# Weight conversion on another engine, two more blocked parts of GEMM 2, and weight tiles shared by alternating rows, in a fused attention and feed-forward kernel

## The chip, the cores and the metric

One core of a Trainium2 chip. The metric is the device time of one execution in microseconds (us), of which the median of several runs is given. TensorE (PE) does matrix products into PSUM, VectorE (DVE), ScalarE (ACT) and GpSimd (POOL) work element by element, and SyncE (SP) starts the transfers between device memory and SBUF. GpSimd can't read PSUM.

## What is computed

Random-feature attention over 8 batches, 8 heads, 576 tokens of 64, and then a feed-forward layer over the 4608 x 512 result:

```python
def phi(x):                                   # x scaled by 64 ** -0.25
    proj = einsum('bhsd,md->bhsm', x, omega)  # 128 features
    h = proj - sum(x * x, -1) / 2
    return exp(h - max(h, -1)) / sqrt(128)
kv = einsum('bhsm,bhsd->bhmd', phi(k), v);  z = sum(phi(k), 2)
x = (phi(q) @ kv) / (phi(q) @ z + 1e-6)       # then to 4608 x 512
h = x @ w_in                                  # GEMM 1: 512 -> 2048
g = h * erf(softplus(h))
out = g @ w_out                               # GEMM 2: 2048 -> 512
```

Inputs and output are float32 but the two weight matrices, which come as float64.

## The kernel before

**Precision.** Each factor of the large products is split in a rounded high part and a rest, both in TensorE's fast float32 format, and each product is three matmuls: high x high, high x rest, rest x high.

**Super-blocks.** The tokens are worked off in six super-blocks (`SUPERS`, line 31) of two halves each, 288, 288, 432, 432, 432 and 432 columns a half. A super-block needs the attention of its tokens to be done, so the attention of later batches (32 pairs of heads) is spread over the GEMMs of earlier super-blocks. GEMM 1 and GEMM 2 go in four quarters q of d_ff; GEMM 2 of a quarter runs beside GEMM 1 of the next (`second`, called with `last`).

**Seven products.** The first three super-blocks do GEMM 1 plainly: for each pair of d_ff tiles and model halves, eight products of blocks. The others take a 2 x 2 block product in seven products (`PRODUCTS`, line 59) of sums of blocks: of the weights S1 to S4, of the right sides T1 to T4. GEMM 2 does the same where `blocked(b, q)` holds: in super-block 4, and in super-block 5 but for its last quarter, seven parts in all. A blocked part makes its right sides in `pieces2`: four differences of half-blocks of g (`gsum`), and high and rest of B21 with B22, of B11, of T1 with T2 and of T3 with T4. It takes its seven products for each of two rows j, whose steps alternate (`merged`).

**Weights.** In super-block 0 each of 32 weight units of 128 x 512 float64 is loaded raw (`st`, as low and high 32-bit words) and turned into float32 by `make` (line 412): `pbias` on ScalarE takes the high word into PSUM with another exponent (`wt`), `ptail` on GpSimd takes the three top bits of the low word, `pjoin` on VectorE shifts one and adds the other bits, `phigh` on ScalarE rounds, `prest` on VectorE subtracts; the result `w` is also stored in device memory (`wdw`). Later uses fetch it from there. The sums S1 to S4 are made by `make_sums` (line 451) from the two weight tiles as they are used in a plain product: those of GEMM 1 in super-block 2, those of GEMM 2 in super-block 3 (`SUMS2`). They are stored too (`wdc`). A blocked product fetches single blocks of 256 KB, and `lease` (line 741) puts two of one row in a tile `wb`, in the groups of `UNITS`.

**Order.** `build` only lists operations with their reads, writes, due times, and possible engines with a duration in us and a slack for each; `Plan.order` (line 151) then simulates the engines with these durations and writes down the order in which every engine's queue gets its instructions. Each queue runs strictly in that order on the chip. Loads are counted as bytes at 270 GB/s and 2.3 us. For the tail the plan has

```python
pl.op("ptail", [("G", 0.95, -1e9)], lambda e: E.w_tail(st), ...
```

Tiles take slots of named pools; `SLOTS` and `CAPS` (lines 78 to 80) bound how many a stream may hold. The pool `w` has 8 slots for weight tiles (`w`, at most 6 up to the end of super-block 3, then 8), raw weights and sums together (`st`, 2), the float32 copies for sums (`wt`, 1) and the rounded sums (`cv`, 2).

Of the kernel before, what the change touches and what calls it, by code (L numbers as in the profile page):

```python
# [14 lines left out]
ALU = mybir.AluOpType  # L15
# [17 lines left out]
FROM = tuple(2 * sum(t for t, _ in SUPERS[:i]) for i in range(len(SUPERS) + 1))  # L33
BLOCKED = 4
SUMS2 = BLOCKED - 1
SUMS = max(i for i, (_, plain) in enumerate(SUPERS) if plain)
# [29 lines left out]
            ("X", "A22", "T4", (1, 0), 0))  # L66
UNITS = (("A11", "S1"), ("S2", "S4"), ("S3", "A12"), ("A22",))


def blocked(b, q):  # L70

    return b >= BLOCKED and (b < len(SUPERS) - 1 or q < NQ - 1)

# [239 lines left out]


AHEAD = 40.0

# [27 lines left out]
def build(emit):  # L344
# [28 lines left out]
    for i in range(len(SUPERS)):  # L373
        starts.append(starts[-1] + per[i] + more[i] * PAIR)

    def pair_time(n, x):
        b, p = divmod(n, NP)
        if b <= need[0]:
            return n * FIRST + x * 14.0
        i = next(i for i in range(len(SUPERS)) if need[i] >= b)  # L380
        each = (starts[i] - starts[i - 1]) / more[i - 1]
        k = (need[i] + 1) * NP - n
        return starts[i] - LEAD - k * each + x * min(each, 33.0) * 1.2
# [18 lines left out]
    def parts(t, src, keys, banked=False):  # L402

        ks = range(2)
        pl.op("phigh" if banked else "whigh", [("A", 0.63, -1e9)] + [("G", 0.7, WHG)] * (not banked),
              lambda e: E.w_high(e, t, src),
              reads=keys, writes=[(t, ("h", k)) for k in ks])
        pl.op("prest" if banked else "wrest", [("V", 0.68, -1e9)] + [("G", 1.3, 3.0)] * (not banked),
              lambda e: E.w_rest(e, t, src),
              reads=keys + [(t, ("h", k)) for k in ks], writes=[(t, ("l", k)) for k in ks])  # L410

    def make(u, t):

        nm = "_".join(str(c) for c in u)
        st = pl.tile("w", f"st{nm}", [P, HW, 2], I32, "st")
        pl.op("wload", [("S", 0.1, AHEAD)], lambda e: E.w_load(st, u),
              writes=[(st, "h"), (st, "l"), (t, "room")], size=P * HW * 8)
        w = pl.tile("ps", f"wt{nm}", [P, HW], I32, "wp")
        pl.op("pbias", [("A", 0.67, -1e9)], lambda e: E.w_bias(e, st, w),
              reads=[(st, "h")], writes=[(w, 0)])  # L420
        pl.op("ptail", [("G", 0.95, -1e9)], lambda e: E.w_tail(st), reads=[(st, "l")], writes=[(st, "l")])
        pl.op("pjoin", [("V", 0.68, -1e9)], lambda e: E.w_join(st, w), reads=[(st, "l"), (w, 0)],
              writes=[(w, 0)])
        parts(t, lambda: w.ap.bitcast(F32).rearrange("p (k c) -> p k c", k=2), [(w, 0)], True)
        store(u, t)

    def room():
        count[0] += 1
        return CAPS["w"] if clock[0] < starts[max(SUMS, SUMS2) + 1] else SLOTS["w"]

# [20 lines left out]
    def make_sums(key, t0, t1):  # L451
# [3 lines left out]
        for i, t in enumerate((t0, t1)):  # L455
            pl.op("wwhole", [("V", 0.68, -1e9), ("G", 1.3, 3.0)],
                  lambda e, i=i, t=t: E.w_whole(e, r.ap[:, i], t),
                  reads=[(t, (x, k)) for x in "hl" for k in range(2)], writes=[(r, i)])
        s = pl.tile("w", "S" + nm, [P, 4, BW], F32, "st")

# [125 lines left out]
    def key_values(n, t0):  # L586
        a = pairs[n]
        f, v = a["fk"], a["v"]
        kvp = a["kvp"] = pl.tile("ps", "kvp" + a["nm"], [P, 512], F32, "att", early(n))
        for j in range(2):  # L590
            pl.op("kv", [("T", (5 - j) * COST["kv"], -1e9)], lambda e, j=j: E.key_values(kvp, f, v, j),
                  reads=[(f, i) for i in range(NC)] + [(v, 0)], writes=[(kvp, 0)],
                  plan=pair_time(n, t0 + 0.08 * j))
        whole = n < WHOLE
        kh = a["kh"] = pl.tile("kh", "kh" + a["nm"], [P, 2, P], F32 if whole else F32R)
        kl = a["kl"] = kh if whole else pl.tile("kl", "kl" + a["nm"], [P, 2, P], F32R)
        pl.op("kvhigh", [("V", 0.6, -1e9), ("A", 0.7, -1e9)], lambda e: E.kv_high(e, kh, kvp),
              reads=[(kvp, 0)], writes=[(kh, 0)])
        if not whole:
            pl.op("kvrest", [("V", 0.6, -1e9)], lambda e: E.kv_rest(kl, kvp, kh),  # L600
                  reads=[(kvp, 0), (kh, 0)], writes=[(kl, 0)])

    def turn(n, t0):
        a = pairs[n]
        whole = n < WHOLE
        lent = ("g", "qh0", 2) if n < NP else ("qh", "qh", None)
# [12 lines left out]
    def attend(n, t0):  # L619
        a = pairs[n]  # L620
        for t, (c0, w) in enumerate(SPANS):
            rc = pl.tile(f"rc{t}", f"rc{a['nm']}_{t}", [P, w])
            nds = [pl.tile("ps", f"nd{a['nm']}_{j}_{t}", [P, 512], F32, "att", early(n)) for j in range(2)]
            for j, nd in enumerate(nds):
                c = range((j * S + c0) // 384, (j * S + c0 + w - 1) // 384 + 1)
                pl.op("nd", [("T", w / 600 if n < WHOLE else 3 * max(0.111, 0.012 + w / 2400), -1e9)],
                      lambda e, j=j, c0=c0, w=w, nd=nd:
# [112 lines left out]

    def lease(where, src, wn):

        if wn not in where:
            us = next(x for x in UNITS if wn in x)
            t = blocks([src(x) for x in us])
            where.update({x: (t, i) for i, x in enumerate(us)})
        return where[wn]

    def gemm1(b, ph, fp):
        T, d = SUPERS[b][0], drain(b)  # L750
        hs = pl.tile("g", f"hs{b}_{ph}_{fp}", [P, 2, 2, T], F32, "hs")
        gran[b, ph, fp] = {"hs": hs}
        where, banks = {}, {}

        def one(bank, wn, xn, to, plus):
            w = lease(where, sources(ph, fp), wn)
            first = bank not in banks
# [98 lines left out]

    def gemm2_blocks(b, q, j):
        T, d = SUPERS[b][0], drain(b)
        where, banks = {}, {}
        src = sources2(q, j)  # L860
        for i in range(2):
# [3 lines left out]
        def one(bank, wn, xn, to, plus):  # L865
            u, k = lease(where, src, wn)
            first = bank not in banks
# [21 lines left out]
    def gemm2(b, q, et):  # L889
# [16 lines left out]
        def one(t, f):  # L906
            if not ops:
                ops.extend(pl.tile("ps", f"o{b}_{q}_{et}_{i}", [P, 512], F32, "moe2",
                                   6 if b == len(SUPERS) - 1 else None) for i in range(2))
                w.append(weights2(q // 2, et, q % 2))  # L910
                if b == SUMS2 and any(blocked(x, q) for x in range(len(SUPERS))):
                    beside[q, et] = w[0]
                    if et >= KH:
                        make_sums(("2", q, et - KH), beside[q, et - KH], w[0])
# [20 lines left out]
    def second(b, q, e):  # L935
        if not blocked(b, q):
            merged([gemm2(b, q, (0, 2, 1, 3)[e])])
        elif not e:
            merged([gemm2_blocks(b, q, j) for j in range(KH)])

# [9 lines left out]
    for b in range(len(SUPERS)):  # L950
        plain = SUPERS[b][1]
        length = (starts[b + 1] - starts[b]) / NQ
        for q in range(NQ):
# [5 lines left out]
            for block in (("f", 0), ("e", 0), ("e", 1), ("e", 2), ("e", 3)):  # L959
                what, x = block  # L960
                if what == "f":
                    gs = range(GP * q, GP * q + GP)
                    merged([(plain1 if plain else gemm1)(b, *divmod(g, FP)) for g in gs])
                    chain(b, gs)
# [12 lines left out]
def tile_attention_moe(ctx: ExitStack, tc: tile.TileContext, qT, kT, qR, kR, qN, kN, vP, omT, w1, w2, out):  # L977
# [68 lines left out]
    class Emit:  # L1046
# [11 lines left out]

        def w_tail(self, t):
            x = t.ap[:, :, 0]  # L1060
            pool.tensor_scalar(x, x.bitcast(mybir.dt.uint32), 2.0 ** -29, 7.0, op0=ALU.mult, op1=ALU.min)

# [288 lines left out]
```

## Time and profile before

| | |
|---|---|
| median of 3 runs | 1058.01 us (1057.6 to 1059.11) |
| profiled execution | 1057.43 us |
| its span, first to last instruction | 1055.6 us, mean granted clock 0.996 |
| TensorE matmul busy | 1028.8 us (97%), 6748 matmuls |
| TensorE weight load busy | 972.6 us (92%) |
| VectorE busy | 786.2 us (74%) |
| ScalarE busy | 690.4 us (65%) |
| GpSimd busy | 617.1 us (58%) |
| DMA | 220.08 MB, 208 GB/s on average |

Matmuls overlap and their ends are modelled, so TensorE's busy time shows where it had nothing to do, not how fast it was. The granted clock is the share of 2.4 GHz that the chip gave TensorE. In the tables of stretches the busy times are in us, in the order matmul, weight load, VectorE, ScalarE, GpSimd. All instructions carry the same line, that of a helper, so groups are told by their tiles: `h`, `hX`, `hY`, `hZ` are banks of GEMM 1, `o`, `oX`, `oY`, `oZ` of GEMM 2, `nd`, `pp`, `pt`, `kvp` of the attention, `hs` and `gs` hold h and its gate, `th`, `tl`, `bh`, `bl`, `bb` right sides of blocked parts, `os` the output sums, `xs` the attention's output, `qh` its turned features, `R` and `S` the float32 copies and the sums of weights. The stretch from 54 to 216 us holds super-block 0 with 26 of the 32 conversions of weights; 340 to 533 is super-block 2, 533 to 733 super-block 3, after that the last two. A wait names what released it last; a queue runs in order, so whatever stands behind a waiting instruction waits as well.

### The profile page before, as it was taken

The page shows a single profiled execution, that of the slowest core. Times are in us where ns is not written, and L with a number is a line of the kernel's source. Part 1 is how long each engine was busy: PE and PEld are TensorE (multiplying, and loading weights), DVE is VectorE, ACT ScalarE, POOL GpSimd, SP SyncE. Part 2 cuts the span into 40 slices and gives each one's busy share as a digit, 9 for nine tenths or more (in the row PEclk, how much of TensorE's full clock was granted, in tenths as well). Part 3 has the DMA queues.
Part 4 walks back from the last instruction along what each step waited for, and adds up shares of the span by engine and source line. Part 5 has one row for each costly group of instructions (what it writes and reads, how often), then busy time and mean ns, then how long its engine had stood idle before and what let it go on. Part 6 is the DMA issues. An engine that isn't in the chain of part 4 may idle for free.

```text
span 1055.6 us, 18596 instructions
## 1 busy us (share of the span) xinstructions
PE 1028.8 (97%) x6748; PEld 972.6 (92%) x6748; DVE 786.2 (74%) x1316; ACT 690.4 (65%) x1300; POOL 617.1 (58%) x436
## 2 busy tenths in 40 slices
PE   7999898999999999999999999999999999999998
PEld 7799788999999999999989999999999999899997
DVE  5767666886777766747787797879887778888664
ACT  8878786776666665664856575758657575635550
POOL 6668756642345755625765264738895688686520
PEclk9999998999999999999999999999999999999999
DMA  8366667587445576446446666666776656677662
GB/s 241 121 207 212 220 244 254 209 308 247 149 160 196 180 238 237 158 159 201 138 156 233 212 214 226 222 202 215 252 268 224 224 179 191 225 267 231 227 209 80
DMA packets 87962, 220.08 MB, mean 208 GB/s; under 512 B 9920, under 2 KB 10432, under 8 KB 87872
## 3 DMA queue, kind: packets, MB, share of 16 engines
q1 hardware_dynamic: 87712, 218.83, 61.8%
q8 instruction: 54, 0.88, 0.4%
q14 instruction: 36, 0.29, 0.1%
q10 hardware_dynamic: 160, 0.07, 0.0%
HBM read 175.87 MB, written 42.99 MB: 207 GB/s over the span
## 4 chain that ended last, share of the span: by engine, by line
PE 82%; DVE 7%; POOL 5%; issue 2%; ACT 2%; DMA 1%; SPq 0%; POOLq 0%; DVEq 0%; ACTq 0%
PE o L994 22%; PE h L994 15%; PE hX L994 9%; PE oX L994 6%; PE kvp L994 5%; PE nd L994 5%; PE ppq L994 4%; PE hY L994 4%; PE ppk L994 4%; PE oY L994 3%; PE hZ L994 2%; PE pt L994 2%; PE oZ L994 1%; POOL st L994 1%; POOL hs L994 1%
## 5 line engine op out<-in xcount | busy, mean ns | idle before, releaser
L994 PE MATMUL o<-gh,w 128*128 128x432 f32 (+1 forms) x1088 | 281.9, 332 | 0.8 <-ACT os L994 0.7
L994 PE MATMUL h<-xh,w 128*128 128x288 f32 (+1 forms) x768 | 199.5, 328 | 3.3 <-DVE w L994 1.9
L994 PEld LDWEIGHTS o<-gh,w 128*128 128x128 f32 x1088 | 192.6, 188 | 6.7 <-ACT os L994 0.9
L994 PE MATMUL o<-gl,w 128*128 128x432 f32 (+1 forms) x544 | 178.7, 329 | 0.1
L994 POOL TENSOR_TENSOR hs<-gs,hs 128x864 f32<-128x864 f32 (+1 forms) x48 | 104.8, 2207 | 87.2 <-ACT gs L994 87.1
L994 PEld LDWEIGHTS h<-xh,w 128*128 128x128 f32 x768 | 135.4, 190 | 9.0 <-DVE w L994 2.9
L994 PE MATMUL hX<-xh,wb 128*128 128x432 f32 x384 | 122.7, 365 | 3.5 <-DVE hs L994 3.4
L994 PE MATMUL h<-xl,w 128*128 128x288 f32 (+1 forms) x384 | 122.1, 318 | 0.1
L994 PEld LDWEIGHTS o<-gl,w 128*128 128x128 f32 x544 | 102.3, 188 | 2.4 <-DVE gl L994 0.4
L994 ACT ACT_TABLE_LOAD x73 | 93.7, 1283 | 2.0 <-PEq L1342 0.7
L994 ACT ACTIVATE fq<-ppq,mxq 128x128 f32<-128x128 f32 x288 | 78.8, 390 | 23.7 <-DVE mxq L994 23.6
L994 POOL TENSOR_TENSOR gl<-hs,gh 128x864 fp32r<-128x864 f32 (+1 forms) x42 | 81.7, 1969 | 15.1 <-DVE gh L994 11.0
L994 POOL TENSOR_TENSOR uk<-uk 128x288 f32<-128x288 f32 (+1 forms) x50 | 39.0, 802 | 84.8 <-DMA uk<-kN 46.4
L994 ACT ACTIVATE fk<-ppk,mxk 128x128 f32<-128x128 f32 x288 | 81.1, 382 | 5.6 <-DVE mxk L994 5.1
L994 DVE TENSOR_TENSOR os<-o,os 128x432 f32<-128x432 f32 (+1 forms) x104 | 55.3, 534 | 39.3 <-PE o L994 38.5
L994 ACT ACTIVATE rc<-nd,eps 64x288 f32<-64x288 f32 x128 | 63.6, 497 | 31.4 <-PE nd L994 29.2
L994 PEld LDWEIGHTS hX<-xh,wb 128*128 128x128 f32 x384 | 72.2, 188 | 9.0 <-DVE hs L994 5.3
L994 POOL TENSOR_SCALAR st<-st 128x512 int32<-128x512 uint32 x32 | 65.9, 2059 | 21.7 <-DMA st<-w 16.6
L994 DVE TENSOR_TENSOR xs<-nd,rc 64x288 f32<-64x288 f32 (+1 forms) x160 | 62.9, 393 | 19.5 <-ACT rc L994 16.4
L994 PEld LDWEIGHTS h<-xl,w 128*128 128x128 f32 x384 | 73.0, 190 | 1.7 <-DVE xl L994 0.3
L994 DVE TENSOR_REDUCE ppk<-ppk 128x4 f32<-128x512 f32 (+1 forms) x72 | 40.5, 563 | 43.2 <-PE ppk L994 42.1
L994 ACT ACTIVATE gs<-hs 128x1728 f32<-128x1728 f32 (+1 forms) x48 | 69.2, 1482 | 0.3
(150 smaller groups left out, 2549.1 us busy)
## 6 DMA issues: line engine op xcount, KB each, us to landing
w<-wdw SPq DMA_DIRECT2D x84, 512.0 KB, 5.6
wb<-wdc SPq DMA_DIRECT2D x152, 256.0 KB, 4.4
wb<-wdw SPq DMA_DIRECT2D x114, 256.0 KB, 4.9
st<-w SPq DMA_DIRECT2D x32, 512.0 KB, 5.4
wdw<-w SPq DMA_DIRECT2D x32, 512.0 KB, 3.8
wdc<-c SPq DMA_DIRECT2D x32, 512.0 KB, 4.2
v<-vP SPq DMA_DIRECT2D x32, 325.0 KB, 4.5
uk<-kR SPq DMA_DIRECT2D x24, 320.0 KB, 3.2
```

The source lines that it names most:

```text
L994: return tc.keep_in_program_order(method(*args, **kwargs))
```

## The change

- `w_tail` may run on VectorE as one logical shift by 29 bits of the low words, in place, and the plan gives it to VectorE alone, at 0.69 us. In a converted unit, rounding (`phigh`) may go to VectorE at 0.66 us besides ScalarE at 0.63.
- `blocked` takes two more parts: quarters 2 and 3 of super-block 3. `FIRST2` names the first blocked super-block of each quarter, and the sums of GEMM 2 are made in the one before it, so those of quarters 2 and 3 move from super-block 3 to super-block 2.
- `lease` makes one tile for each name of a block, holding it for both of the two alternating rows (two tiles of d_ff in GEMM 1, two rows j in GEMM 2), instead of tiles that hold two blocks of one row. `UNITS` goes.
- Raw weights get 3 buffers and sums a stream of their own with 1; weight tiles may hold 6 slots until super-block 2 begins, 5 through super-blocks 2 and 3, then 8.
- `WHOLE2`, `STARTS` and `whole_` are added with values that leave everything as it was.

```diff
-BLOCKED = 4
-SUMS2 = BLOCKED - 1
...
-UNITS = (("A11", "S1"), ("S2", "S4"), ("S3", "A12"), ("A22",))
+FIRST2 = (4, 4, 3, 3)
 def blocked(b, q):
-    return b >= BLOCKED and (b < len(SUPERS) - 1 or q < NQ - 1)
+    return FIRST2[q] <= b < len(SUPERS) - (q == NQ - 1)
...
-CAPS = dict(st=2, wt=1, wp=2, cv=2, att=4, moe1=5, moe2=3, hs=4, gs=2, w=6)
+CAPS = dict(st=3, wt=1, ws=1, wp=2, cv=2, att=4, moe1=5, moe2=3, hs=4, gs=2, w=6, wsums=5)
...
+TAIL = [("V", 0.69, -1e9)]
...
-        pl.op("phigh" if banked else "whigh", [("A", 0.63, -1e9)] + [("G", 0.7, WHG)] * (not banked),
+        pl.op("phigh" if banked else "whigh", [("A", 0.63, -1e9), ("V", 0.66, -1e9) if banked else ("G", 0.7, WHG)],
...
-        pl.op("ptail", [("G", 0.95, -1e9)], lambda e: E.w_tail(st), reads=[(st, "l")], writes=[(st, "l")])
+        pl.op("ptail", TAIL, lambda e: E.w_tail(e, st), reads=[(st, "l")], writes=[(st, "l")])
...
-        return CAPS["w"] if clock[0] < starts[max(SUMS, SUMS2) + 1] else SLOTS["w"]
+        if clock[0] < starts[SUMS]:
+            return CAPS["w"]
+        return CAPS["wsums"] if clock[0] < starts[max(SUMS + 1, *FIRST2)] else SLOTS["w"]
...
-        s = pl.tile("w", "S" + nm, [P, 4, BW], F32, "st")
+        s = pl.tile("w", "S" + nm, [P, 4, BW], F32, "ws")
...
-    def lease(where, src, wn):
+    def lease(where, srcs, wn, i):
         if wn not in where:
-            us = next(x for x in UNITS if wn in x)
-            t = blocks([src(x) for x in us])
-            where.update({x: (t, i) for i, x in enumerate(us)})
-        return where[wn]
+            where[wn] = blocks([src(wn) for src in srcs])
+        return where[wn], i
...
-                if b == SUMS2 and any(blocked(x, q) for x in range(len(SUPERS))):
+                if b == FIRST2[q] - 1:
...
-            merged([gemm2_blocks(b, q, j) for j in range(KH)])
+            where, srcs = {}, [sources2(q, j) for j in range(KH)]
+            merged([gemm2_blocks(b, q, j, where, srcs) for j in range(KH)])
...
-        def w_tail(self, t):
+        def w_tail(self, e, t):
             x = t.ap[:, :, 0]
+            if e == "V":
+                dve.tensor_scalar(x, x, 29, None, op0=ALU.logical_shift_right)
+                return
             pool.tensor_scalar(x, x.bitcast(mybir.dt.uint32), 2.0 ** -29, 7.0, op0=ALU.mult, op1=ALU.min)
```

## Rows read from the trace of the kernel before

**Rows 1.** Busy time by stretch: stretch, length, each engine (instructions), granted clock, DMA, GB/s.

```profile
54.00:216.00 162.00, 151.84 (x1156) 145.38 (x1156) 112.70 (x209) 126.73 (x253) 107.55 (x74) 0.98 0.67 231
...
160.00:165.00 5.00, 2.23 (x7) 1.98 (x8) 1.90 (x4) 2.81 (x9) 4.76 (x5) 0.54 0.77 275
...
340.00:533.00 193.00, 193.00 (x1232) 182.74 (x1231) 133.39 (x220) 125.41 (x222) 115.46 (x88) 1.00 0.57 191
533.00:733.00 200.00, 199.44 (x1283) 185.74 (x1282) 162.71 (x290) 128.52 (x263) 107.14 (x85) 1.00 0.62 206
733.00:798.00 65.00, 64.70 (x390) 60.51 (x389) 55.29 (x85) 38.63 (x70) 57.54 (x39) 1.00 0.78 268
798.00:1055.00 257.00, 249.69 (x1330) 235.83 (x1329) 192.10 (x241) 139.93 (x175) 148.69 (x76) 1.00 0.61 203
```

**Rows 2.** TensorE in order of time: start, duration, operation, [idle before, releaser].

```profile
115.79 0.40 PE L994 MATMUL h<-xh,w 128*128 128x288 f32 x1 [0.93 <-DVE w L994]
...
118.68 1.24 PE L994 MATMUL nd<-qh,kh 128*128 128x288 f32 x4 [0.50 <-DVE qh L994]
...
120.46 0.40 PE L994 MATMUL h<-xh,w 128*128 128x288 f32 x1 [0.54 <-ACT w L994]
...
129.14 0.37 PE L994 MATMUL h<-xh,w 128*128 128x288 f32 x1 [0.85 <-DVE xs L994]
...
162.77 1.30 PE L994 MATMUL nd<-qh,kh 128*128 128x288 f32 x2 [4.45 <-DVE qh L994]
```

**Rows 3.** The chain that ended last, in order of time: start, duration, what.

```profile
159.46 1.98 POOL st L994
161.47 0.04 DVE wt L994
...
162.07 0.56 DVE qh L994
...
162.77 1.30 PE nd L994 x2
164.07 2.88 PE h L994 x12
...
169.31 1.98 PE h L994 x15
...
918.11 2.36 PE oY L994 x12
```

**Rows 4.** Waits by pair, 40 to 225 us: in total, times, longest.

```profile
POOL st L994 <- DMA st<-w: 16.6, 9, 3.7
DVE wt L994 <- POOL st L994: 10.6, 9, 2.1
...
ACT wt L994 <- DMA st<-w: 4.7, 2, 2.6
```

**Rows 5.** Groups by shape: operation, shapes, count | busy, mean ns | idle before.

```profile
L994 POOL TENSOR_SCALAR st<-st 128x512 int32<-128x512 uint32 x32 | 65.9, 2059 | 21.7 <-DMA st<-w 16.6 <-PE ppq L994 1.8 <-DVE hs L994 1.5
...
L994 POOL TENSOR_TENSOR R<-w 128x512 f32<-128x512 f32 x19 | 25.9, 1374 | 9.7 <-DMA w<-wdw 4.2 <-PE hX L994 4.1 <-POOL xc L994 0.7
...
L994 DVE TENSOR_TENSOR os<-oX,os 128x432 f32<-128x432 f32 x44 | 26.1, 603 | 20.2 <-PE oX L994 20.1
...
L994 DVE TENSOR_TENSOR gs<-hs,gs 128x864 f32<-128x864 f32 x7 | 15.0, 2140 | 0.8 <-POOL hs L994 0.8
...
L994 DVE CAST xh<-xs 128x432 fp32r<-128x432 f32 x6 | 2.5, 420 | 1.8 <-PE hX L994 1.2 <-PE h L994 0.5
```

**Rows 6.** VectorE in order of time, the gate alone.

```profile
108.09 1.36 DVE L994 TENSOR_TENSOR hs<-gs,hs 128x1152 f32<-128x1152 f32 x1 [2.98 <-ACT gs L994]
...
152.14 2.54 DVE L994 TENSOR_TENSOR hs<-gs,hs 128x1152 f32<-128x1152 f32 x1
```

**Rows 7.** Raw weights, tile st: ns min/median/max, first and last start; loads below.

```profile
L994 DVE SCALAR_TENSOR_TENSOR wt<-wt,st x32: 682/699/700, 22.8 to 221.3; 128x512 int32<-128x512 int32 x32
...
DMA to landing us min/median/max: 3.3/5.4/10.5
```

More of the change, by code (lines that the diff above doesn't have):

```diff
@@ L312, in order, with whole_ @@
         return out
+def whole_(n):
+    return n < WHOLE or WHOLE2[0] <= n < WHOLE2[1]
 AHEAD = 40.0
@@ L321 @@
 WHOLE = 8
+WHOLE2 = (0, 0)
 LESS = []
@@ L331 @@
 EARLY = (0, 0)
+STARTS = ()
 VOS = 5
+TAIL = [("V", 0.69, -1e9)]
 LATE = 40.0
@@ L374, in build @@
         starts.append(starts[-1] + per[i] + more[i] * PAIR)
+    if STARTS:
+        starts = list(STARTS)
     def pair_time(n, x):
@@ L593, in key_values @@
                   plan=pair_time(n, t0 + 0.08 * j))
-        whole = n < WHOLE
+        whole = whole_(n)
         kh = a["kh"] = pl.tile("kh", "kh" + a["nm"], [P, 2, P], F32 if whole else F32R)
@@ L604, in turn @@
         a = pairs[n]
-        whole = n < WHOLE
+        whole = whole_(n)
         lent = ("g", "qh0", 2) if n < NP else ("qh", "qh", None)
@@ L625, in attend @@
                 c = range((j * S + c0) // 384, (j * S + c0 + w - 1) // 384 + 1)
-                pl.op("nd", [("T", w / 600 if n < WHOLE else 3 * max(0.111, 0.012 + w / 2400), -1e9)],
+                pl.op("nd", [("T", w / 600 if whole_(n) else 3 * max(0.111, 0.012 + w / 2400), -1e9)],
                       lambda e, j=j, c0=c0, w=w, nd=nd:
@@ L739, in plain1, with gemm1 @@
         return [lambda i=i, t=t: one(i, t) for i in range(2) for t in range(2)]
-    def lease(where, src, wn):
+    def lease(where, srcs, wn, i):
         if wn not in where:
-            us = next(x for x in UNITS if wn in x)
-            t = blocks([src(x) for x in us])
-            where.update({x: (t, i) for i, x in enumerate(us)})
-        return where[wn]
-    def gemm1(b, ph, fp):
+            where[wn] = blocks([src(wn) for src in srcs])
+        return where[wn], i
+    def gemm1(b, ph, fp, where, srcs, which):
         T, d = SUPERS[b][0], drain(b)
@@ L752, in gemm1 @@
         gran[b, ph, fp] = {"hs": hs}
-        where, banks = {}, {}
+        banks = {}
         def one(bank, wn, xn, to, plus):
-            w = lease(where, sources(ph, fp), wn)
+            w = lease(where, srcs, wn, which)
             first = bank not in banks
@@ L855, in keep, with gemm2_blocks @@
               plan=clock[0] + 3.0, size=P * 2 * SUPERS[b][0] * 4)
-    def gemm2_blocks(b, q, j):
+    def gemm2_blocks(b, q, j, where, srcs):
         T, d = SUPERS[b][0], drain(b)
-        where, banks = {}, {}
-        src = sources2(q, j)
+        banks = {}
         for i in range(2):
@@ L865, in one @@
         def one(bank, wn, xn, to, plus):
-            u, k = lease(where, src, wn)
+            u, k = lease(where, srcs, wn, j)
             first = bank not in banks
@@ L962, in build @@
                     gs = range(GP * q, GP * q + GP)
-                    merged([(plain1 if plain else gemm1)(b, *divmod(g, FP)) for g in gs])
+                    if plain:
+                        merged([plain1(b, *divmod(g, FP)) for g in gs])
+                    else:
+                        where, srcs = {}, [sources(*divmod(g, FP)) for g in gs]
+                        merged([gemm1(b, *divmod(g, FP), where, srcs, i) for i, g in enumerate(gs)])
                     chain(b, gs)
```

## The prediction

> **What bounds the kernel now.** I read the stage table first [rows 1]. From 216 us to the end TensorE is hardly ever idle: 0 of 193 us in 340:533, 0.6 of 200 in 533:733, 0.3 of 65 in 733:798, 7.3 of 257 in the last stage. There the time is the number of matmuls times their pitch, and other engines matter only when they run late. The exception is 54:216, in which all the weights are made and super-block 0 is computed: TensorE is idle for 10.2 us of 162 there. So two questions remain: how many matmuls go, and which idle time of that stage goes.
>
> The idle times of TensorE [rows 2] answer half of the second. Eight gaps between 115 and 163 us, 8.28 us together, stand behind the making of weights (five are shown; three more, 0.62, 0.20 and 0.19 us, are like the first). There are three kinds: TensorE waits for the weight itself (`w`, five gaps, 2.48 us), or for `qh` (0.50 and 4.45 us), or for `xs` (0.85 us). The last two are not weights. The chain of waits shows why they count [rows 3]: before the 4.45 us gap ends, GpSimd runs a tail (`st`, 159.46 to 161.44), VectorE's join `wt` starts at 161.47, and only then the copy `qh` at 162.07, which stands behind the join in VectorE's queue. The waits by pair say the same in total [rows 4]: VectorE's joins waited 10.6 us for GpSimd's tails, nine times.
>
> The reason is in the group of the tail [rows 5]: 2.06 us each on GpSimd, 32 times, while the plan that writes the order of all queues assumes 0.95 us. The order is made for a chain that is 1.1 us shorter than it is.
>
> The long gap also slows the clock: in 160:165 the granted clock is 0.54 [rows 1], between the levels of 1.2 and 2.4 GHz, after 4.45 idle us. From 162.77 on 14 matmuls of 288 columns take 1.30 + 2.88 = 4.18 us; a little later 15 take 1.98 us, 0.132 each [rows 3]. At that pitch the 14 would take 1.85: the clock cost 2.3 us.
>
> **The change, part by part.**
>
> *Seven products in two more parts of d_ff* (super-block 3, quarters 2 and 3). A plain part has 4 output tiles x 2 halves x 4 slices x 3 = 96 matmuls of 432 columns; a blocked one has 7 products x 2 x 2 x 3 = 84. So 24 matmuls go. Their pitch in the dense stage is 2.36 us for 12, 0.197 each [rows 3]: **-4.7 us**. They stand in stages without idle time, so all of it is on the path.
>
> What comes for it, beside TensorE: per part four differences of half-blocks, 2592 more elements per lane to round and to subtract, and six more evictions (14 for 8). If all of it but the rounding went to VectorE at the row of the differences (2.14 us for 864 elements): 4 x 2.14 + 2592 x 2.48 ns + 6 x 0.60 = 18.6 us [rows 5], twice. In return four of the eight sums of GEMM 2 leave 533:798 for super-block 2: ten instructions each, at most 1.37 us [rows 5], up to 13.7 us a sum, and two stores on SP's queue, which move with it. So this stretch keeps its load (VectorE 218 of 265 us, GpSimd 165), and 340:533 takes at most 55 us more on two engines that now stand idle for 60 and 78 us of it [rows 1]. I take 0. Bounds: the last stage has seven blocked parts and 7.3 idle us [rows 1]; were all of it theirs, 1.0 a part, +2.1 for two; the other way -0.3, the idle time of 733:798, where sums of quarter 3 are now made. If the cover fails, the differences are late and TensorE waits for `th` and `tl`.
>
> The bytes: 28 more block loads of 256 KB for eight loads of 512 KB, 3 MB of 220. Hidden, since no transfer is ever what TensorE waits for. *Shared tiles*: of each pair of alternating rows one tile now holds the same block, so it is used up within two neighbouring products, where before a tile with S2 and S4 stayed from the third product to the sixth. Five tiles (before six) in super-blocks 2 and 3 then hold more work ahead. I take 0; below nothing it can't go by much, as no wait on these loads is there to be removed; above, it would show as TensorE waiting for `wb`, for which no row speaks. A third buffer for raw weights and a place of its own for sums take the two that this frees.
>
> *The tail on VectorE.* 26 of the 32 tails lie in 54:216. GpSimd loses 26 x 2.06 = 53.6 of its 107.6 us; VectorE gets 26 shifts of 128x512. No row shows one. Nearest is the join, which reads the same strided words: 0.70 us [rows 7]; a cast from SBUF to SBUF of 432 elements takes 0.42 us [rows 5], so the bounds are 0.4 and, should it be held up as below, 1.9 us. I take 0.68, +17.7 us. *Rounding on VectorE* for ScalarE, whichever is free first: 0.69 us by the join's row; for half of 26, +9.0 us (none: 0; all: 17.9). VectorE then has 112.7 + 26.7 = 139.4 of 162 us (86%, before 70%). It stays below full, but what is queued behind on it (`qh`, `xs`, evictions, maxima) comes later at times.
>
> Why that is worth time: the tail's place in the plan becomes true (0.69 planned, some 0.7 run), and the join follows the shift in the same queue instead of waiting for GpSimd. Term by term: the 0.50, 0.85 and 4.45 us gaps and the 2.3 us of clock go, 8.1 us; of the 2.5 us in which the weight itself is late about half goes, as the chain gets 1.4 us shorter a tile, 1.2 us; late next is VectorE, 16 points fuller, for which I give back 2.3 us (between 0 and 10.6, which is all of the 8.28 and 2.3). Sum **-7.0 us**.
>
> One rule speaks against this part. An SBUF-to-SBUF operation on VectorE can be held up by GpSimd: the gate of 1152 elements took 1.36 us at 108.09 with GpSimd idle, and 2.54 us at 152.14 beside GpSimd's own gate [rows 6], 1.18 us more. The joins, which read one operand from PSUM, stay between 0.68 and 0.70 [rows 7].
> The Trainium skill has this as a rule ("SBUF — State Buffer", section "Who interferes with whom"): VectorE and GpSimd share a port pair, "an exclusive lock", and a one-input operation from SBUF to SBUF in a two-port mode takes it as well. By it the shift would pay this, where the join before did not; the time that gives is rival 3.
>
> **Sum.** The profiled execution took 1057.43 us (span 1055.6). 1057.4 - 4.7 - 7.0 = 1045.7: **1046 us**, -1.1%. The median of the runs shown, 1058.01, is 0.6 above the profiled one; on it the sum would be 1046.3.
>
> **Rivals.**
>
> 2. Only the matmuls go. The order of every queue is written anew, and 54:216 gets other gaps of nearly the same total: VectorE is in everything TensorE waits for, and it gets fuller. For it: the plan was wrong in more than the tail. Against it: nine of the long waits name this one figure. 1057.4 - 4.7 and at most a quarter of the 7.0: 1051 to 1053, say 1052.
>
> 3. VectorE becomes the bound of 54:216. All roundings go to it and each of 26 shifts is held up by 1.18 us: 112.7 + 26 x (0.68 + 0.69 + 1.18) = 179 of 162 us, 17 over. TensorE's loss there would be 17 for 10.2 + 2.3; +4.5, less the 4.7 of the matmuls: 1057.2, no change. Against it: GpSimd has half its work left in that stage, so there is less to collide with.
>
> 4. VectorE inherits the wait for the load; slower. GpSimd's tails waited 16.6 us in nine waits for the raw weights (1.85 us each) [rows 4]: the plan counts 4.2 us for a load (512 KB at its 270 GB/s, and 2.3), the median is 5.4 and the longest 10.5 us [rows 7]. GpSimd could bear that; on VectorE every eviction stands behind it. Of VectorE's 10.6 us of waiting for tails 8.3 came through to TensorE, 0.78. A wait costs 1.85 x 0.78 = 1.44 us. What can be gained, 4.7 + 8.3 + 2.3 = 15.3, is used up at 10.6 waits: from 11 waits of 26 on the kernel is slower. At 18 it is 1057.4 - 15.3 + 26.0 = 1068. For it: nine waits were there already. Against it: a third raw buffer lets loads start earlier, and ScalarE, which reads the same load first, waited for it only twice [rows 4].
>
> That the matmuls don't go can't be: the code fixes their number.
>
> **Chances.** Forecast 0.62 (its own range 1039 to 1051: 1040.2 if all 10.2 + 2.3 us go with the 4.7, and 1 us more if a new order also fills some of the last stage's 7.3; 1051 if 1.7 of 7.0 remain); rival 2 0.18; rival 3 0.08; rival 4 0.12. 0.2%, about 2 us, is what a measurement of this kernel can tell from no change. Faster 0.80 (the first two), the same 0.08, slower 0.12. The range is 1039 to 1058: it takes in rivals 2 and 3 and leaves out the fourth.
>
> **What would show it.** Right: 24 matmuls of 432 columns fewer and no new idle time in 340:798; no joins waiting for GpSimd; shifts of 0.4 to 0.7 us; under 5 us idle and a full clock in 54:216. Wrong: shifts above 1.2 us (rival 3); VectorE waiting for `st` loads more than ten times (rival 4); TensorE waiting for `wb`, `w` loads, `th` or `tl` after 340 us; a 54:216 stage with the same 10 us idle under other names (rival 2).

## The result, and the profile after

| | median us (executions) | lowest to highest | ratio to before, 95% |
|---|---|---|---|
| before, beside the first runs | 1057.95 (4) | 1057.6 to 1059.11 | |
| changed kernel | 1045.56 (4) | 1041.34 to 1050.42 | 0.988 [0.986, 0.990] |
| changed kernel, taken again | 1042.45 (4) | 1041.78 to 1046.8 | 0.9863 [0.9847, 0.9879] |

Forecast was 1046 us. The kernel got 1.2 to 1.4% faster. All eight executions together have a median of 1043.4 us and lie 9.1 us apart, where the kernel before varies by 2.5 to 5.0 in 22 to 29 executions beside the experiments: no step of the prediction has this. Of the other kernels below `tail_only`, `round_act`, `st2` and `old_lease` vary by 10 to 14 us too, `no_blk` by 2.3. One execution of `round_act` (1063.82 us) counts as slow and is left out of the medians and ratios below. The first profile is of the longest execution (1050.42 us, span 1048.5), the second of one of the shortest (1041.80 us, span 1039.9). Both are used below.

The stage table of the first, in the columns of [rows 1]:

```profile
54.00:216.00 162.00, 158.00 (x1227) 152.63 (x1227) 132.22 (x258) 127.56 (x257) 63.31 (x58) 1.00 0.68 237
160.00:165.00 5.00, 5.00 (x37) 4.79 (x36) 3.19 (x10) 3.68 (x12) 0.00 (x0) 1.00 0.99 345
340.00:533.00 193.00, 193.00 (x1210) 182.62 (x1208) 140.69 (x225) 122.76 (x231) 119.61 (x92) 1.00 0.58 202
533.00:733.00 200.00, 194.58 (x1250) 181.46 (x1249) 169.38 (x295) 131.60 (x258) 130.77 (x109) 0.98 0.64 217
733.00:798.00 65.00, 65.00 (x390) 61.03 (x391) 55.23 (x84) 39.78 (x77) 38.03 (x23) 1.00 0.75 256
798.00:1049.00 251.00, 243.21 (x1294) 230.37 (x1290) 187.36 (x228) 135.62 (x160) 137.69 (x74) 1.00 0.59 202
```

Against [rows 1], 54:216 has lost 6.2 of its 10.2 idle us, at a full clock, and the stretch around 160 us is full. 340:533 and 733:798 have no idle time, and from 798 on it is 7.8 us for 7.3. But 533:733 has 5.4 idle us where it had 0.6, and a granted clock of 0.98. In the second profile that stretch is whole:

```profile
533.00:733.00 200.00, 199.53 (x1303) 186.42 (x1303) 169.75 (x303) 134.47 (x267) 142.08 (x113) 1.00 0.67 228
```

TensorE's gaps over 0.3 us in 110:164 of the first profile, in the columns of [rows 2]; the second has the same five within 0.04 us:

```profile
114.41 0.55 PE L1008 MATMUL pt<-ident,fq 128*128 128x128 f32 x3 [0.35 <-DVE os L1008]
118.04 0.40 PE L1008 MATMUL h<-xh,w 128*128 128x288 f32 x1 [0.52 <-ACT qh L1008]
151.51 0.37 PE L1008 MATMUL h<-xh,w 128*128 128x288 f32 x1 [0.91 <-DVE w L1008]
155.39 0.40 PE L1008 MATMUL h<-xh,w 128*128 128x288 f32 x1 [0.79 <-ACT w L1008]
157.01 0.53 PE L1008 MATMUL h<-xh,w 128*128 128x288 f32 x2 [1.09 <-DVE w L1008]
```

Together 3.66 us. The same count gives 8.84 us before (the prediction's 8.28 leave out a gap of 0.95 us before `pt` and take in two short ones); the 4.45 us gap before `nd` [rows 2] is gone. The new operation by itself, and the waits of VectorE's joins, answering to [rows 5] and [rows 4]. First the group of the shifts in 54:216 (count | busy, mean ns | idle before):

```profile
L1008 DVE TENSOR_SCALAR st<-st 128x512 int32<-128x512 int32 x27 | 16.4, 610 | 1.0 <-DMA st<-w 0.8
```

then all 32 in the view of their tile (ns min/median/max):

```profile
L1008 DVE TENSOR_SCALAR st<-st x32: 409/430/1624, 17.9 to 212.6; 128x512 int32<-128x512 int32 x32
```

and the waits by pair in 54:216 (total, times, longest):

```profile
DVE wt L1008 <- ACT wt L1008: 7.5, 6, 2.2
ACT w L1008 <- DVE wt L1008: 4.2, 5, 1.6
```

The shift alone takes 0.43 us; held up it takes up to 1.62, and its mean is 0.61. No join waits for GpSimd any more; the longest waits of that chain are now for ScalarE's first step.

### The profile page after: what moved, and what is told of

The parts are those of the page before. It is cut to its first block, busy times and chain, and to the rows that moved or that the text cites. A ratio compares the mean times of both kernels' runs of the same rounds, so it can differ in the third digit from the quotient of the medians.

```text
span 1048.5 us, 18562 instructions
## 1 busy us (share of the span) xinstructions
PE 1024.2 (98%) x6724; PEld 970.4 (93%) x6724; DVE 816.8 (78%) x1361; ACT 688.9 (66%) x1291; POOL 572.3 (55%) x437
## 4 chain that ended last, share of the span: by engine, by line
PE 82%; DVE 8%; ACT 4%; DMA 2%; issue 2%; POOL 1%; SPq 0%; ACTq 0%; DVEq 0%; POOLq 0%
PE o L1008 20%; PE h L1008 15%; PE hX L1008 10%; PE oX L1008 6%; PE kvp L1008 5%; PE hY L1008 5%; PE nd L1008 4%; PE ppq L1008 4%; PE ppk L1008 3%; PE oY L1008 3%; PE hZ L1008 3%; PE pt L1008 2%; DMA st<-w 2%; PE oZ L1008 2%; ACT gs L1008 1%
## 5 line engine op out<-in xcount | busy, mean ns | idle before, releaser
L1008 PE MATMUL o<-gh,w 128*128 128x288 f32 (+1 forms) x960 | 243.4, 328 | 0.0
L1008 PE MATMUL h<-xh,w 128*128 128x288 f32 (+1 forms) x768 | 197.1, 326 | 3.5 <-DVE w L1008 2.0
L1008 PEld LDWEIGHTS o<-gh,w 128*128 128x128 f32 x960 | 168.5, 188 | 4.6
L1008 POOL TENSOR_TENSOR hs<-gs,hs 128x864 f32<-128x864 f32 (+1 forms) x46 | 96.4, 2119 | 122.2 <-ACT gs L1008 112.4
L1008 PE MATMUL o<-gl,w 128*128 128x288 f32 (+1 forms) x480 | 155.8, 325 | 0.1
L1008 PEld LDWEIGHTS o<-gl,w 128*128 128x128 f32 x480 | 90.4, 188 | 2.1 <-DVE gl L1008 0.5
L1008 ACT ACTIVATE fq<-ppq,mxq 128x128 f32<-128x128 f32 x288 | 79.0, 389 | 10.8 <-DVE mxq L1008 10.3
L1008 POOL TENSOR_TENSOR uq<-uq 128x288 f32<-128x288 f32 (+1 forms) x44 | 38.2, 889 | 87.6 <-DMA uq<-qN 49.8
L1008 POOL TENSOR_TENSOR gl<-hs,gh 128x576 fp32r<-128x576 f32 (+1 forms) x42 | 72.2, 1747 | 23.7 <-ACT gh L1008 21.6
L1008 ACT ACTIVATE gs<-gs 128x1728 f32<-128x1728 f32 (+1 forms) x48 | 69.0, 1481 | 0.3
L1008 PE MATMUL hX<-xl,wb 128*128 128x432 f32 x192 | 68.8, 358 | 0.0
```

The lines of the kernel that those rows point to most:

```text
L1008: return tc.keep_in_program_order(method(*args, **kwargs))
```

## Where TensorE's time went

For 54:216 the table takes idle time as 162 minus the busy time of TensorE in the stage row, and the loss of clock as 162 times what the granted clock lacks of 1.00 (good to 0.8 us, since the row has two digits). Where TensorE is idle while its clock is low, both terms count it: before, in 160:165. So the sum is an upper bound of what was lost. "After 520" is the sum of TensorE's idle times from there to the end. Each in the profiled execution of the kernel; the medians are of the executions.

The last column is when the last plain matmul of GEMM 1 starts, of which some expectations below speak. In all fourteen profiles 3586 matmuls stand up to it, so by then the same work is done, while of a stretch with fixed ends a faster kernel does more. From the view of tile `h` (count: ns min/median/max, first and last start), before, `tail_round`, `tail_both` and the changed kernel:

```profile
L994 PE MATMUL h<-xh,w x768: 288/297/855, 42.6 to 507.3; 128*128 128x288 f32 x128, 128*128 128x432 f32 x64
L994 PE MATMUL h<-xh,w x768: 288/297/855, 45.9 to 505.8; 128*128 128x288 f32 x128, 128*128 128x432 f32 x64
L994 PE MATMUL h<-xh,w x768: 288/297/514, 44.1 to 498.0; 128*128 128x288 f32 x128, 128*128 128x432 f32 x64
L1008 PE MATMUL h<-xh,w x768: 288/297/514, 45.4 to 499.2; 128*128 128x288 f32 x128, 128*128 128x432 f32 x64
```

| kernel | edit | median (n), low to high | ratio, 95% | 54:216 idle + clock | idle after 520 | last plain |
|---|---|---|---|---|---|---|
| before | | 1057.95 (4) | | 10.2 + 3.2 | 8.8 | 507.3 |
| changed | all | 1043.4 (8), 1041.3 to 1050.4 | 0.988, 0.9863 | 4.0 + 0 | 12.7; 7.8 | 499.2; 498.8 |
| `tail_only` | before, tail to VectorE | 1059.45 (12), 1055.5 to 1066.1 | 1.0017 [0.9998, 1.0035] | 7.4 + 3.2 | 12.0 | 506.4 |
| `tail_true` | before, tail planned 2.06 us | 1059.68 (12), 1057.0 to 1063.6 | 1.0014 [1.0003, 1.0024] | 9.1 + 3.2 | 9.6 | 508.3 |
| `round_only` | before, rounding may go to VectorE | 1060.36 (11), 1057.1 to 1062.0 | 1.002 [1.0011, 1.003] | 11.4 + 6.5 | 9.4 | 511.0 |
| `tail_round` | before, tail and rounding | 1050.36 (6), 1049.2 to 1055.5 | 0.9936 [0.992, 0.9952] | 5.9 + 4.9 | 5.3 | 505.8 |
| `tail_both` | the same, third raw buffer | 1049.06 (6), 1047.7 to 1053.3 | 0.9928 [0.9911, 0.9944] | 3.9 + 0 | 8.6 | 498.0 |
| `blk_only` | before, two blocked parts | 1055.68 (12), 1054.6 to 1059.8 | 0.9983 [0.9974, 0.9992] | 10.3 + 3.2 | 9.2 | 508.3 |
| `no_blk` | changed, without them | 1051.77 (6), 1051.0 to 1053.3 | 0.9944 [0.9932, 0.9956] | 4.0 + 0 | 10.5 | 498.6 |
| `round_act` | changed, rounding on ScalarE | 1052.19 (11), 1046.1 to 1060.5 | 0.9958 [0.9938, 0.9978] | 8.7 + 1.6 | 10.1 | 509.7 |
| `st2` | changed, two raw buffers | 1054.06 (11), 1048.3 to 1059.3 | 0.9963 [0.9943, 0.9983] | 6.3 + 4.9 | 10.0 | 503.2 |
| `old_lease` | changed, weight tiles of one row | 1055.76 (12), 1051.2 to 1061.2 | 0.9981 [0.9963, 0.9998] | 3.9 + 1.6 | 17.5 | 499.6 |
| `gap_pool` | changed, small writes on GpSimd | 1043.71 (4), 1043.3 to 1044.9 | 0.9868 [0.9855, 0.9881] | 4.0 + 0 | 10.5 | 497.4 |

The parts don't add up. Put into the kernel before, one at a time, they are worth +1.5 (tail; not told from none), +2.3 (rounding) and -2.2 us (blocked parts); left out of the changed kernel, one at a time, 8.4 to 12.4 us each, for a whole gain of 14.5. The column "idle after 520" is a warning: edits that touch nothing after 520 us move the idle time there between 5.3 and 12.0. Every edit lets the planner write all queues anew; but two executions of the one changed program lie as far apart as 12.7 and 7.8, so how much of this is the new order isn't known.

## The experiments

**Is it the tail's place in the plan?** `tail_only` moves the shift and nothing else; `tail_true` leaves it on GpSimd and gives the plan its true time.

```diff
 # tail_only, against before (and the shift in w_tail)
-pl.op("ptail", [("G", 0.95, -1e9)], lambda e: E.w_tail(st), ...
+pl.op("ptail", [("V", 0.69, -1e9)], lambda e: E.w_tail(e, st), ...
 # tail_true, against before
+pl.op("ptail", [("G", 2.06, -1e9)], lambda e: E.w_tail(st), ...
```

> The kernel before with one edit: the tail of the weights runs on VectorE as a shift, planned at 0.69 us; rounding stays on ScalarE, tiles and blocked parts are as before. Theory (the tail on GpSimd, longer than planned, made the gaps of 54 to 216 us): the gain of that stage comes with this edit alone, 1058 - 7 = 1051 us (1048 to 1054), with the joins no longer waiting for GpSimd. Rival (the third raw buffer, the shared tiles or the rounding are needed for it): 1056 us or more, and the gaps before nd and h stay.

> The kernel before with one figure of the plan changed: the tail stays on GpSimd, but is planned at the 2.06 us it takes, not 0.95. If the wrong figure was the whole cause, the order written with the right one gets at least half of the 7 us: 1051 to 1054 us, and the joins wait for GpSimd less than 3 us in all. If GpSimd is too slow for the chain whatever the order, 1056 us or more, with the weight itself late (waits of h on w) in place of waits behind the join.

Neither gains. In `tail_true` VectorE's joins still wait 5.4 us for GpSimd, five times, and `h` waits for the weight itself, as its second branch had it: a true figure in the plan doesn't make the chain shorter. In `tail_only` the 4.45 us gap goes, but others come:

```profile
113.17 0.41 PE L994 MATMUL o<-gh,w 128*128 128x288 f32 x1 [2.17 <-DVE w L994]
...
156.57 0.55 PE L994 MATMUL pt<-ident,fq 128*128 128x128 f32 x3 [1.50 <-DVE hs L994]
159.56 0.40 PE L994 MATMUL h<-xh,w 128*128 128x288 f32 x1 [1.84 <-ACT w L994]
```

The stage loses 10.6 us for 13.4, not 4, and a gap of 3.74 us at 870 (below) takes more than that back. That profile is of an execution of 1061.35 us; six of the twelve lie between 1055.5 and 1057.6, just below the kernel before, six between 1061.3 and 1066.1. At the last plain matmul the kernel is 0.9 us ahead. The theory that the tail alone is what 54:216 was waiting for falls.

**Which of the other edits does it take?** `round_only` and `tail_round` add to the kernel before; `round_act` and `st2` take from the changed one; `tail_both` has tail, rounding and buffer without blocked parts and shared tiles.

```diff
 # round_only, tail_round, tail_both, against before; round_act takes it back
-pl.op("phigh" ..., [("A", 0.63, -1e9)] + [("G", 0.7, WHG)] * (not banked),
+pl.op("phigh" ..., [("A", 0.63, -1e9), ("V", 0.66, -1e9) if banked else ("G", 0.7, WHG)],
 # tail_both, against before (and S goes to the stream ws); st2 has st=2 in the changed kernel
-CAPS = dict(st=2, wt=1, wp=2, ...
+CAPS = dict(st=3, wt=1, ws=1, wp=2, ...
```

> The kernel before with one edit: rounding of converted weights may go to VectorE. The tail stays on GpSimd, planned at 0.95 us. Tail and rounding together gave 1050.4 us, the tail alone nothing. If the rounding alone is the gain (ScalarE was the bound of the chain, and the tail's move is idle), 1050 to 1052 us. If both are needed, because VectorE's queue still waits for GpSimd's tails, 1055 us or more, with the joins waiting for tails 8 us or more in all.

> The kernel before with tail and rounding on VectorE as in the change, two raw buffers and the old tiles, caps and blocked parts. If the rounding is what the tail alone lacked, 1050 to 1052 us and the last plain matmul of GEMM 1 at 499 to 501 us; if the third buffer is, no gain over the tail alone: 1056 to 1060 us, 505 us or later.

> The kernel before with tail and rounding on VectorE, three raw buffers and the sums in a place of their own; tiles for blocked products, weight slots and blocked parts as before. If these three edits are the whole gain of 54 to 216 us, this equals the changed kernel without its two parts: 1050 to 1053 us, the last plain matmul of GEMM 1 at 499 to 501 us. If the shared tiles and the slots are needed too, 1055 us or more.

> The changed kernel with the rounding of converted weights on ScalarE alone; all else of the change stays. The tail alone gained nothing (1059.5 us), so something else of the change makes the gain of 54 to 216 us. If it is the rounding on VectorE (ScalarE is the fullest engine of that stage, 127 of 162 us), this is slower than the changed kernel by 5 us or more, 1051 us up, with the last plain matmul of GEMM 1 (499.2 us in the changed kernel, 507.3 before) at 504 us or later. If it is the third raw buffer, it stays at 1046 us and 500 us.

> The changed kernel with two raw buffers in place of three (sums keep their own place). If the third buffer makes the gain of 54 to 216 us, 1051 us or more and the last plain matmul of GEMM 1 at 504 us or later; if the rounding makes it, 1046 us and 500 us.

At the last plain matmul `round_only` is 3.7 us behind the kernel before (its joins wait 7.3 us for tails, four times), `tail_round` 1.5 ahead, `tail_both` 9.3, as far as the changed kernel (8.1 and 8.5). Taken from the changed kernel, the buffer costs 4.0 us there and the rounding 10.5, of which up to 5.1 is clock: 0.68, 0.50 and 0.79 were granted in the three 5 us from 30 us on, 1.00 in every other profile. `tail_round` has the median that was expected if the rounding is what the tail lacked, but 5.6 of the 7.1 us by which its profile is shorter come behind 507 us, where its edits change no more than the order of the queues.

Row of 54:216 of `tail_both`:

```profile
54.00:216.00 162.00, 158.10 (x1229) 152.88 (x1228) 130.40 (x257) 127.52 (x256) 63.09 (x57) 1.00 0.69 237
```

and of `st2`, which differs from the changed kernel in the third raw buffer only:

```profile
54.00:216.00 162.00, 155.71 (x1181) 150.44 (x1180) 127.33 (x245) 127.39 (x240) 58.75 (x52) 0.97 0.65 227
```

With all three edits 54:216 loses 4 us (5.5 in `old_lease`, below); without the rounding or without the buffer 10.3 to 11.2; without tail and buffer 17.9. All six profiles with tail, rounding and third buffer (`tail_both`, `no_blk`, `old_lease`, `gap_pool`, the changed kernel twice) have the five gaps of 110:164 shown above, within 0.1 us, and their last plain matmul at 497.4 to 499.6 us; the other eight have neither. The buffer with the rounding but not the tail was not run, so that the tail is needed beside them isn't shown. What the buffer changes can be read from `st2`: from its timeline, first TensorE's gaps, then VectorE ahead of the second of them.

```profile
115.72 0.75 PE L1008 MATMUL nd<-qh,kh 128*128 128x288 f32 x2 [1.43 <-ACT qh L1008]
...
156.02 0.75 PE L1008 MATMUL nd<-qh,kh 128*128 128x288 f32 x2 [2.01 <-DVE qh L1008]
...
152.04 0.52 DVE L1008 TENSOR_SCALAR st<-st 128x512 int32<-128x512 int32 x1
152.66 0.70 DVE L1008 SCALAR_TENSOR_TENSOR wt<-wt,st 128x512 int32<-128x512 int32 x1
153.26 0.69 DVE L1008 TENSOR_REDUCE ppk<-ppk 128x4 f32<-128x512 f32 x1
153.86 1.63 DVE L1008 TENSOR_SCALAR st<-st 128x512 int32<-128x512 int32 x1
155.42 0.55 DVE L1008 COPY qh<-pt 128x384 f32<-128x384 f32 x1
```

In `st2` the copy `qh` stands behind the join and a shift that was held up to 1.63 us. In the changed kernel, at the same place, it stands between two shifts, ahead of the held one:

```profile
152.02 0.52 DVE L1008 TENSOR_SCALAR st<-st 128x512 int32<-128x512 int32 x1
152.46 0.55 DVE L1008 COPY qh<-pt 128x384 f32<-128x384 f32 x1
152.93 1.18 DVE L1008 TENSOR_SCALAR st<-st 128x512 int32<-128x512 int32 x1
154.03 1.28 DVE L1008 SCALAR_TENSOR_TENSOR wt<-wt,st 128x512 int32<-128x512 int32 x2
```

So a gap before `nd` comes back at 2.01 us with two buffers. `tail_round`, also with two, has it at 2.00, and 1.43, 0.77 and 0.96 for the three before it in `st2` (1.43, 0.75, 0.95): it is the order that two buffers get, not one execution. Why the plan puts `qh` there is not shown. `tail_both` is better than `tail_round` by 6.9 us in this stage and by 7.8 at the last plain matmul, but their profiled executions are only 2.8 us apart and their medians 1.3: `tail_round` idles 3.3 us less after 520. The rest is open.

**What are the blocked parts worth?** `blk_only` puts the two parts into the kernel before (with the pool's bounds that hang on them), `no_blk` takes them from the changed one.

```diff
 # no_blk, against the changed kernel
-FIRST2 = (4, 4, 3, 3)
+FIRST2 = (4, 4, 4, 4)
 # blk_only, against before
-    return b >= BLOCKED and (b < len(SUPERS) - 1 or q < NQ - 1)
+    return FIRST2[q] <= b < len(SUPERS) - (q == NQ - 1)
```

> The kernel before with the two more blocked parts alone (and the sums of quarters 2 and 3 in super-block 2); tail on GpSimd, tiles, caps and rounding as before. Theory (24 matmuls at 0.197 us, all else hidden): 1058 - 4.7 = 1053.3 us (1052 to 1055). Rival (the old tiles and caps can't feed the blocked parts, so the gain hangs on the shared tiles): 1056 us or more, with new idle time of TensorE between 340 and 800 us.

> The changed kernel with the blocked parts as before (seven), all sums of GEMM 2 in super-block 3; the tail on VectorE, the rounding, the shared tiles and the caps stay. Theory: 24 matmuls come back, 1045.6 + 4.7 = 1050.3 us (1049 to 1052). Rival (the two parts bring new gaps that eat part of their matmuls): less than 3 us slower than the changed kernel, under 1048.6 us, and the idle times of the changed kernel's trace at 543, 720 and 827 us (1.7, 3.3 and 1.5 us) are gone here.

The span less TensorE's idle time and less the loss of clock, both over the whole run (the clock from rows of 5 us), is 1022.7 to 1026.4 us in the seven profiles with seven parts (1024.9 before and in `tail_both`, 1026.4 in `no_blk`), and 1018.6 to 1021.2 in the seven with nine (1020.3 and 1019.7 in the changed kernel, 1021.2 in `blk_only`, 1019.9 in `gap_pool`): 5.1 us between the means, near the 4.7 of the forecast. `no_blk` lies in the range of its theory. In the median `blk_only` shows only 2.2 us, between its theory and its rival; as the rival had it, its row of 733:798 shows new idle time, 1.9 us at a clock of 0.97:

```profile
733.00:798.00 65.00, 63.14 (x373) 58.59 (x370) 51.80 (x84) 40.89 (x74) 47.73 (x31) 0.97 0.71 235
```

**Are the shared tiles free?** `old_lease` gives the changed kernel tiles of two blocks of one row again.

```diff
-        if wn not in where:
-            where[wn] = blocks([src(wn) for src in srcs])
-        return where[wn], i
+        if (wn, i) not in where:
+            us = next(x for x in UNITS if wn in x)
+            t = blocks([srcs[i](x) for x in us])
+            where.update({(x, i): (t, k) for k, x in enumerate(us)})
+        return where[wn, i]
```

> The changed kernel with the old tiles for blocked products (two blocks of one row in a tile, in the old groups); five weight slots in super-blocks 2 and 3 stay, so do the nine blocked parts. Theory of the prediction (shared tiles hide more loads, but nothing was waiting): 1045 to 1047 us. Rival (five slots with long-lived tiles starve TensorE): 1050 us or more, with new gaps after 524 us, at hX to oZ, while up to 500 us it is as the changed kernel.

It loses 12 of 14.5 us, and its fastest of 12 executions is 10 us above the fastest of the changed kernel. Up to 220 us it idles as the changed one does; the loss is later:

```profile
706.08 0.43 PE L1011 MATMUL oY<-th,wb 128*128 128x432 f32 x1 [0.92 <-PE pt L1011]
709.54 0.47 PE L1011 MATMUL oX<-th,wb 128*128 128x432 f32 x1 [0.52 <-DVE os L1011]
721.89 0.47 PE L1011 MATMUL oZ<-bh,wb 128*128 128x432 f32 x1 [3.04 <-DVE os L1011]
738.77 0.55 PE L1011 MATMUL pt<-ident,fq 128*128 128x128 f32 x3 [1.01 <-DVE hs L1011]
...
865.69 0.37 PE L1011 MATMUL nd<-qh,kh 128*128 128x288 f32 x1 [3.20 <-DVE qh L1011]
```

The time and the place are those of the rival, but not its cause: none of them waits for a weight tile. The two long ones are the mechanism of the next experiment, which this profile meets twice, the changed kernel's once and not at all. Whether the old tiles do that, or an order of the queues that happens to be worse, is not shown: `blk_only` has the old tiles with six slots for weights and nine blocked parts, and no idle time over 2.1 us after 220. Old tiles with six slots and the other edits were not run. `no_blk`, with shared tiles, and `tail_both`, without, are 2.7 us apart the other way: with seven parts nothing speaks for the shared tiles.

**Why do executions of one program differ by 9 us?** The same program again, and the changed kernel with a write of one column after every step on GpSimd.

```diff
+    gap = const.tile([P, 1], F32, name="gap")
 ...
     o.fn(o.eng)
+    if o.eng == "G":
+        pool.memset(gap, 0.0)
```

> The changed kernel once more, unchanged, for its spread (1041.3 to 1050.4 us in four runs) and a second trace. If its runs differ by how long VectorE is held up behind runs of GpSimd operations, a trace of a faster run lacks the 3.3 us gap at 720 us, and the longest VectorE operation on 1728 elements between 700 and 730 us takes under 4 us there instead of 6.3. If the loads make the spread, the gaps differ by what TensorE waits for weights.

> The changed kernel with a memset of one column (0.1 us, writes only) behind every operation of the plan on GpSimd, some 430, which breaks its unbroken runs. Theory (VectorE gets the shared port only when GpSimd's run of operations ends, and this makes the late gaps and the spread): no VectorE operation of 1728 elements over 5 us, spread under 5 us, median 1040 to 1044 us. Rival (spread and late gaps come from elsewhere): the spread stays at 9 us, 1045 us or a few more for 43 us more work on GpSimd.

From the timeline of the first profile, first VectorE, then GpSimd, then TensorE:

```profile
712.69 0.61 DVE L1008 TENSOR_TENSOR os<-oY,os 128x432 f32<-128x432 f32 x1
713.22 6.33 DVE L1008 TENSOR_TENSOR hs<-gs,hs 128x1728 f32<-128x1728 f32 x1
719.47 0.60 DVE L1008 TENSOR_TENSOR os<-oX,os 128x432 f32<-128x432 f32 x1
...
712.41 1.29 POOL L1008 TENSOR_TENSOR uk<-uk 128x288 f32<-128x288 f32 x2
713.66 4.07 POOL L1008 TENSOR_TENSOR hs<-gs,hs 128x864 f32<-128x864 f32 x2
...
720.63 0.73 PE L1008 MATMUL oZ<-bh,wb 128*128 128x432 f32 x1 [3.28 <-DVE os L1008]
```

and the row of the 5 us behind that gap, as in [rows 1]:

```profile
720.00:725.00 5.00, 4.37 (x13) 4.11 (x14) 3.92 (x8) 0.94 (x2) 2.18 (x2) 0.50 0.00 0
```

The same instructions of the same queues in the second profile, VectorE, then GpSimd:

```profile
710.98 2.29 DVE L1008 TENSOR_TENSOR hs<-gs,hs 128x1728 f32<-128x1728 f32 x1
713.19 0.59 DVE L1008 TENSOR_TENSOR os<-oX,os 128x432 f32<-128x432 f32 x1
...
710.12 1.33 POOL L1008 TENSOR_TENSOR uk<-uk 128x288 f32<-128x288 f32 x2
711.38 6.65 POOL L1008 TENSOR_TENSOR hs<-gs,hs 128x864 f32<-128x864 f32 x2
```

That the second, faster execution lacks the 3.28 us gap and the long gate is what its expectation had. In one VectorE's gate takes 6.33 us and GpSimd's two 4.07, in the other 2.29 and 6.65: one of the two waits for the other. In the first VectorE does not get its turn between GpSimd's instructions but only when their unbroken run is over, at 717.73, and ends 1.82 us later. Three evictions stand behind it, TensorE waits 3.28 us for the second of them (`oZ`), and the granted clock of 720:725 is 0.50, the level of 1.2 GHz. The same sum, the end of GpSimd's run plus 1.82 us for 1728 elements, gives the end of `tail_only`'s longest, which waits behind seven instructions in a row; VectorE's, the last of GpSimd's, and TensorE's gap:

```profile
860.49 9.36 DVE L994 TENSOR_TENSOR bl<-hs,bh 128x1728 fp32r<-128x1728 f32 x1
...
866.95 1.08 POOL L994 TENSOR_TENSOR xc<-xs,xc 128x432 f32<-128x432 f32 x1
...
870.38 0.40 PE L994 MATMUL nd<-ql,kh 128*128 128x288 f32 x1 [3.74 <-DVE ql L994]
```

(868.03 and 1.82 make 869.85), and of the two instructions of VectorE ahead of the long gaps of `old_lease`:

```profile
714.89 6.43 DVE L1011 TENSOR_TENSOR hs<-gs,hs 128x1728 f32<-128x1728 f32 x1
...
858.44 6.64 DVE L1011 TENSOR_TENSOR bb<-hs,bb 128x864 fp32r<-128x864 f32 x1
```

GpSimd's runs end there at 719.51 and 864.16, VectorE's instructions at 721.32 and 865.08: 1.81 us, and 0.92 for half the elements. The kernel before has short cases of it already, one behind two of GpSimd's instructions, where 432 elements should take 0.46 us:

```profile
530.15 4.10 DVE L994 TENSOR_TENSOR xl<-xs,xh 128x432 fp32r<-128x432 f32 x1
```

The other new gap of the first profile, 1.70 us at 543.09, is put down to "issue", but ends 0.46 us after a difference on VectorE of 3.30 us, in the second profile 1.94, that ended 1.83 us after GpSimd's.

`gap_pool` is steadier, 1.6 us between its extremes, and no VectorE instruction in its profile takes over 4 us. That is what its theory expected. It is no proof that the writes did this: the second profile of the changed kernel and those of eight other kernels have no such instruction either, there are four executions, the gate at 711 got its turn between two instructions that have no such write between them, and the gap at 541 is there again (1.72 us). It is no faster than the changed kernel's median and not as fast as that kernel's best. So that VectorE can wait behind an unbroken run of several instructions is shown, five times; what decides who gets the turn, and that this is all of the spread, is not.

## Why the prediction was right or wrong

- **Matmuls: right.** 6724 for 6748, forecast 4.7 us, measured about 5.
- **The size of 54:216: right; its cause: wrong.** Forecast -7.0; the stage row gives -9.4 (13.4 to 4.0), the last plain matmul -8.1 and -8.5. The step that failed is "the tail's place in the plan becomes true". A true place alone gives 1 us of the stage (`tail_true`), the tail on VectorE alone 2.8 (`tail_only`); at the last plain matmul the one is 1.0 us behind and the other 0.9 ahead. The third buffer was costed at nothing and the rounding as a mere load; without either the stage keeps 10 to 11 us, as rival 2 had it, with a `qh` in the list again. Tail, rounding and buffer together give it (`tail_both`, 9.5 us of the stage). [rows 3] had shown an obstacle, a `qh` behind a join in VectorE's queue, which is also what `st2` shows; I took the wait of the join for the cause and not the place in the queue.
- **VectorE's load: right but for one thing.** The shifts take 16.4 us for 17.7, rounding is 12 for 13 at 0.68. The sum, 132.2 us of 162 for 139.4, is lower because four `gl` (7.9 us) have left VectorE for GpSimd, which the prediction didn't have. The shift runs near the low bound, 0.43 in the median, and being held up adds 0.18 on the mean; GpSimd is busy for 63.3 us in place of 107.6. Rival 3's price, 1.18 us, is that of the longest shift (1.62 less 0.43); fourteen of 32 take over 0.5 us, three over 1.2.
- **Rival 4 didn't come:** VectorE waited for loads of raw weights 0.8 us in this stage, twice, not eleven times.
- **Shared tiles at 0: open.** Left out, with five slots kept, they cost 12 us, and not through a wait for `wb`, the only sign that I looked for. Whether the tiles or the new order did this is not shown.
- **No new idle time in 340:798: half right.** True in the second profile (0.5 us in 533:733), not in the first (5.4). The load of 533:798 is nearly kept, as forecast (VectorE 224.6 us for 218.0, GpSimd 168.8 for 164.7). Rival 3's mechanism was looked for in 54:216 alone; 3.3 of the 5.4 idle us that the first profile has in 533:733 come from it. The bound of +2.1 us was too low for single executions. That the blocked parts bring this is not shown: `tail_only` has the longest case without the two new parts, and the second profile has them without it.

That the total came out at 1046 is thus partly luck: a stage better than forecast by 1 to 2.4 us, for another reason than the one given, against up to 8.6 us that some executions lose and others of the same program don't.

## What to carry to other kernels

In a queue with a fixed order look for what stands behind the late instruction, and try the edits together before one of them is named the cause. When a planner rewrites every queue, one edit's time also holds the new order of all the rest, and here single executions differ by several us as well. So read the stage and not the median alone, and better, read when a fixed amount of work is done. Long VectorE instructions with both operands in SBUF should not meet a run of GpSimd instructions without a break; bound such a meeting by the run's length, not by one instruction.

## What was not expected of the hardware

- VectorE waited for whole runs of GpSimd's instructions, up to 9.36 us for work of 1.82 us. The Trainium skill ("SBUF — State Buffer", section "Who interferes with whom") has the pair locked by whoever issues first, for the whole instruction. The lock agrees with every row above; that the one who waits may be passed over at the end of each instruction is what these runs add.
- The shift of 512 strided 32-bit words takes 0.43 us where the join, on the same words and PSUM, takes 0.69 and GpSimd's form of it took 2.06.
- One gap of 3.28 us late in the kernel went with a granted clock of 0.50 in the 5 us from 720 and 0.85 in the next five: together 3.2 us of clock, as much again as the gap. But `old_lease` and `tail_both` have the same gaps in 110:164, within 0.02 us, and 155:160 has a clock of 0.66 in the one and 1.00 in the other. What decides that is not shown.
